# A fused attention and MLP kernel: token mixing of the first batch by head pair instead of by token tile, with the token weights transposed ahead of the first PV

## The chip, the cores and the metric

The kernel runs on one core of one Trainium2 chip. Its time is the device time of one execution in microseconds; for a kernel it is the median of several executions. The engines are called as in the profile: PE is TensorE (matmuls; PEld its weight loads), DVE is VectorE, ACT is ScalarE, POOL is GpSimd, SP is SyncE, which here only issues DMAs. POOL issues DMAs too.

## The reference

For each of 8 batches and 8 heads (576 tokens, head dimension 64) attention with a window of 32 to both sides and 8 global tokens; the result, with the heads side by side, is x (8, 576, 512). Then a residual MLP block with affine layers:

```python
scores = scale * q @ k.T ;  scores = where(mask, scores, -1e9)
mask = (abs(pos_i - pos_j) <= 32) | is_global_i | is_global_j
x  = softmax(scores) @ v                       # (8, 576, 512)
a1 = alpha1 * x + beta1
u  = x + lam * einsum('ts,bsd->btd', w_tok, a1)  # token mixing, w_tok (576, 576)
a2 = alpha2 * u + beta2
out = u + lam * (relu(a2 @ w_ch1) @ w_ch2)     # w_ch1 (512, 2048), w_ch2 (2048, 512)
```

Inputs and output are float32; the kernel multiplies in bf16 and fp16 and sums in float32.

## The kernel before

The program is one stream of instructions per engine, in the order in which the Python code issues them; waits between engines come from the tiles that they share. The order of the work is written out by hand. PSUM has eight banks of 128 x 512 float32, handed out in rings: `mlp_ps` banks 0 to 2, `sc_ps` banks 3 and 4, `pv_ps` banks 5 to 7. A ring hands a bank out again only when what was read from it before has been read, so PE waits where a copy out of a bank is late.

**Units of attention.** Heads go in four pairs (hp 0 to 3), each of 128 columns. `tr_pair` turns Q and K of a pair by PE transposes (L556) and copies them to `QP` and `KT`; `glob` picks the global columns. `sc_unit(b, hp, u)` makes a third of a pair's scores, their exp on ACT (L294, tile E), and in its last third the masked copies on DVE (PGQ, L301; PT, L306). `gk_all` and `g_rows` make the rows of the global keys (G, L249). `gq_pv` multiplies the global queries' part (RG: ACT L321, then DVE L322). `pv_x` and `pv_y` are the PV product of a pair for token tiles 0 to 2 and for tile 3 with the 64 last tokens; DVE takes the reciprocal (L347) and normalises (L354) into `XR` (tiles 0 to 3) and `SR` (the last 64 tokens). `xl_eng(b)`, which is POOL, then multiplies x by `LA1` (alpha1 times lam) into the bf16 tiles `XL` and `XL4` (L372, L398, L402), the input of token mixing.

**Token mixing.** w_tok is loaded to `WTB` and transposed to `wtT` by six `wtok_tr(k)`: five PE transposes into a bank of `mlp_ps` and one ACT copy each (L727, L729). The term of beta1 is carried by one more row: `b0_beta` writes lam times beta1 into a row of XL4 (L717, POOL), and matmuls with `ones` sum the columns of wtT into a bank (`psr`, `psr2`), from which ACT copies the sums into row 64 of chunk 4 of `wtT` and row 0 of `wt4o`. `tok_tile(b, i)` then makes one tile of 128 tokens and all 512 columns by five matmuls of 512 columns, `finish_u` adds x on DVE (L411). For batch 0 the result is transposed on PE by four float32 transposes (L418), and DVE multiplies by alpha2 (`a2c`, L420) into `UT[0]`, the input of the MLP; for the other batches POOL multiplies (L426) and a DMA transposes.

**MLP.** The 36 tiles of 128 tokens go in nine groups of four. `mlp(g)` lists 128 items: items 0 to 63 are the W1 matmuls (16 column blocks ec, four chunks cc; a chunk cc of UT is the 128 columns of a head pair), with one ReLU on ACT after each fourth (L484, with the tile `bias1`); items 64 to 127 are W2, and DVE multiplies by lam and adds u (L499, L500). `bias1` is beta2 times W1, made by 64 one-column matmuls. `weave` lays the attention of the next batch and its token mixing between the items of a group: parts are given as (units, first item, last item). For group 0 this is `first_attention(1)`, whose Q and K are cast by `cast_k` (POOL) and `cast_q` (DVE) and transposed on PE.

**The part before group 0** is a list of `run(...)` calls (L753 to L769) for batch 0, followed by the sums, the bias, the casts and token mixing (L771 to L795). POOL's queue in this part, in order: V loads of batch 1 (`load_v`, L199), the first `b0_beta`, pair 2's XL, both loads of W2 (`ld_w2`, L631), pair 3's XL, the second `b0_beta`, `cast_k`.

Of the kernel before, what the change touches and what calls it, by code (L numbers as in the profile page):

```python
# [9 lines left out]
FP32 = mybir.dt.float32  # L10
# [6 lines left out]
P = 128  # L17
# [72 lines left out]
def kernel(ctx, tc, q, k, v, global_idx, alpha1, beta1, w_tok, alpha2, beta2, w_ch1, w_ch2, lam, out):  # L90
# [78 lines left out]
    abr = T("abr", [8, P], FP32)  # L169
    a2c = T("a2c", [P, 4], FP32)  # L170
    b2c = T("b2c", [P, 4], BF16)
    ones = T("ones", [P, P], BF16)
    gbc = T("gbc", [P, 8], FP32)
    gsel = T("gsel", [P, 8], FP32)
# [178 lines left out]
        rb = bass.AP(rr.tensor, rr.offset, [rr.ap[0], [2, n], [1, 2], [0, 64]])  # L353
        nc.vector.tensor_tensor(out=xo, in0=pv[:, :, :, 0:64], in1=rb, op=ALU.mult)  # L354

    def xl_eng(b):
        return nc.gpsimd

    def pv_x(b, hp):
        st = {}  # L360

        def tile_i(i):
            def f():
                if i == 0:
                    st["ps"] = pv_ps()
                pv_mms(b, hp, i, st["ps"][:, 130 * i : 130 * i + 130])
                if i == 2:
                    base = 4 * (b % 3)
                    xo = XR[:, base : base + 3, 128 * hp : 128 * hp + 128]
                    norm(st["ps"], recip(st["ps"], 3), 0, 3, 0, P, xo.rearrange("p i (a d) -> p i a d", a=2))  # L370
                    l = LA1[:, 128 * hp : 128 * hp + 128]
                    xl_eng(b).tensor_tensor(  # L372
                        out=XL[b % 2][:, 0:3, 128 * hp : 128 * hp + 128],
                        in0=xo,
                        in1=bass.AP(l.tensor, l.offset, [l.ap[0], [0, 3], [1, 128]]),
                        op=ALU.mult,
                    )

            return (0.75, f)

        return [tile_i(i) for i in range(3)]

    def pv_y(b, hp):
        st = {}
        par = b % 2
        cs = slice(128 * hp, 128 * hp + 128)

        def f3():
            st["ps"] = pv_ps()
            pv_mms(b, hp, 3, st["ps"][:, 0:130])  # L390

        def f4():
            ps = st["ps"]
            pv_mms(b, hp, 4, ps[:, 130:260])
            xo = XR[:, 4 * (b % 3) + 3, cs]
            rt = recip(ps, 2)
            norm(ps, rt, 0, 1, 0, P, xo.rearrange("p (i a d) -> p i a d", i=1, a=2))
            xl_eng(b).tensor_tensor(out=XL[par][:, 3, cs], in0=xo, in1=LA1[:, cs], op=ALU.mult)  # L398
# [3 lines left out]
            xl_eng(b).tensor_tensor(out=XL4[par][r0 : r0 + 64, cs], in0=xo, in1=LA1[r0 : r0 + 64, cs], op=ALU.mult)  # L402

        return [(0.75, f3), (0.4, f4)]

    nub = [0]
    late = []

    def finish_u(t, ps):
        x = xs(t)  # L410
        nc.vector.tensor_tensor(out=x, in0=ps, in1=x, op=ALU.add)  # L411
        g, j = PLACE[t]
        js = slice(128 * j, 128 * j + 128)
        if t[0] == 0:

            def tail():
                for cc in range(4):
                    nc.tensor.transpose(out=ps[:, 128 * cc : 128 * cc + 128], in_=x[:, 128 * cc : 128 * cc + 128], identity=ident)  # L418
                ab = bass.AP(a2c.tensor, a2c.offset, [a2c.ap[0], [1, 4], [0, 128]])
                nc.vector.tensor_tensor(out=UT[g % 2][:, :, js], in0=ps.rearrange("p (c t) -> p c t", c=4), in1=ab, op=ALU.mult)  # L420

            late.append(tail)
            return
        ub = UB[nub[0] % 4]
        nub[0] += 1
        nc.gpsimd.tensor_tensor(out=ub, in0=x, in1=A2, op=ALU.mult)  # L426
        nc.sync.dma_start_transpose(out=UT[g % 2][:, :, js], in_=ub)

    def tok_tile(b, i):
        par = b % 2  # L430

        def f():
# [40 lines left out]
    def mlp(g):  # L473
        ut = UT[g % 2]
        a = []
        st = {}

        def w1(ec, cc):
            def f():
                if cc == 0:  # L480
                    st["ps"] = mlp_ps()
                mm(st["ps"], W1[:, cc, ec * P : (ec + 1) * P], ut[:, cc, :], cc == 0, cc == 3)
                if cc == 3:
                    nc.scalar.activation(out=HT[:, ec, :], in_=st["ps"], func=AF.Relu, bias=bias1[:, ec : ec + 1], scale=1.0)  # L484
# [24 lines left out]
        for ec in range(16):  # L509
            for cc in range(4):  # L510
                a.append(w1(ec, cc))
# [252 lines left out]
    nc.tensor.transpose(out=psb[:, 0:8], in_=abr, identity=ident[0:8, 0:8])  # L764
    nc.vector.tensor_copy(out=b2c, in_=psb[:, 0:4])
    nc.vector.tensor_copy(out=a2c, in_=psb[:, 4:8])
# [9 lines left out]
    nc.scalar.copy(out=wtT[64:65, 4, 64:576], in_=psr[64:65, :])  # L776
    nc.scalar.copy(out=wtT[64:65, 4, 0:64], in_=psr2[64:65, 0:64])
    nc.scalar.copy(out=wt4o[0:1, 64:576], in_=psr[0:1, :])
    nc.scalar.copy(out=wt4o[0:1, 0:64], in_=psr2[0:1, 0:64])
    psb = mlp_ps()  # L780
    for ec in range(16):
        for cc in range(4):
            mm(psb[:, ec : ec + 1], W1[:, cc, ec * P : (ec + 1) * P], b2c[:, cc : cc + 1], cc == 0, cc == 3)
    nc.vector.tensor_copy(out=bias1, in_=psb[:, 0:16])
# [12 lines left out]
    def first_attention(b):  # L797
# [106 lines left out]
```

The softmax here doesn't subtract the row's maximum and nothing guards it: scores larger than these inputs give would overflow.

## Time and profile before

| | us |
|---|---|
| median of 7 runs | 407.79 (406.36 to 408.64) |
| profiled execution, its own time | 407.58 |
| its span, first to last instruction | 405.7 |
| PE busy | 374.1 (92%) |
| DVE, POOL, ACT busy | 229.9, 210.8, 167.5 |
| first PV matmul starts | 31.91 |
| first token mixing matmul starts | 47.57 |
| first MLP matmul starts | 56.90 |
| first matmul of group 1 starts | 104.55 |

The span is that of the profiled execution. A row of the timeline or of the chain gives the start in microseconds from the span's beginning, the length, the engine, the line of the code (L117 is the helper `mm`, so all its matmuls have that line and are told apart by their tiles), and in brackets how long the engine stood before and who ended that. A matmul's length includes the time that its result needs to leave the array, so in a row of equal matmuls it is the distance of the starts that counts.

### The profile page before, as it was taken

How to read it: one execution, taken by the hardware profiler on the slowest of the kernel's cores; microseconds unless marked ns; L12 is line 12 of the kernel's file. 1: busy time of each engine (PE TensorE's matmuls, PEld its weight loads, DVE VectorE, ACT ScalarE, POOL GpSimd, SP SyncE). 2: the span in 40 equal slices, each digit the busy share in tenths (PEclk: the TensorE clock that was granted, in tenths of full speed). 3: DMA queues.
4: the chain of work that ended last, by engine and by line, in shares of the span. 5: the costliest groups of instructions: out<-in, count | busy, mean ns of one | idle time of the engine just before them, and what ended most of it. 6: DMA issues, size and time to landing. Idle time of an engine off the chain costs nothing.

```text
span 405.7 us, 8036 instructions
## 1 busy us (share of the span) xinstructions
PE 374.1 (92%) x3017; PEld 211.2 (52%) x3071; DVE 229.9 (57%) x621; ACT 167.5 (41%) x318; POOL 210.8 (52%) x282
## 2 busy tenths in 40 slices
PE   0658889999899999999999999999999999999996
PEld 0547556654465456545654565456545654444443
DVE  3775487579455846694569456845694565113013
ACT  2644317710573067206730772067207810540720
POOL 9534929554973994489438863894331334100000
PEclk9996899999999999999999999999999999999999
DMA  9999999992999999799949999999522003201002
GB/s 151 249 235 241 133 204 104 144 145 65 144 148 146 138 143 130 119 131 144 143 108 134 131 134 148 111 150 134 123 63 79 2 26 76 68 2 78 27 27 78
DMA packets 161690, 48.25 MB, mean 119 GB/s; under 512 B 147530, under 2 KB 154770, under 8 KB 161652
## 3 DMA queue, kind: packets, MB, share of 16 engines
q0 software_dynamic: 98752, 16.99, 60.7%
q1 hardware_dynamic: 62100, 30.36, 39.1%
q8 instruction: 24, 0.39, 0.4%
q10 hardware_dynamic: 800, 0.39, 0.4%
q14 instruction: 14, 0.11, 0.1%
HBM read 39.28 MB, written 9.44 MB: 120 GB/s over the span
## 4 chain that ended last, share of the span: by engine, by line
PE 85%; DMA 8%; DVE 3%; POOL 2%; issue 1%; ACT 1%; DVEq 0%; POOLq 0%; ACTq 0%
PE bank L117 84%; DMA XR<-in_k_dram 5%; DMA XR<-in_q_dram 3%; DVE QP L560 1%; PE bank L556 1%; POOL XL L372 0%; POOL Ve L199 0%; PE bank L418 0%; DVE OT L539 0%; POOL XL L717 0%; ACT QP L560 0%; POOL XL L402 0%; DVE XR L500 0%; POOL W L631 0%; PE bank L241 0%
## 5 line engine op out<-in xcount | busy, mean ns | idle before, releaser
L117 PE MATMUL bank<-UT,W 128*128 128x512 bf16 x545 | 153.5, 379 | 3.1 <-issue 1.1
L117 PE MATMUL bank<-W,HT 128*128 128x512 bf16 (+2 forms) x574 | 137.6, 373 | 0.8 <-issue 0.2
L484 ACT ACTIVATE HT<-bank,bias 128x512 bf16<-128x512 f32 x144 | 98.8, 687 | 66.3 <-PE bank L117 65.6
L294 ACT ACTIVATE E<-bank 128x416 f16<-128x416 f32 (+1 forms) x96 | 47.5, 514 | 122.8 <-PE bank L117 121.9
L117 PEld LDWEIGHTS <-HT 128*128 128x128 bf16 x592 | 53.4, 98 | 53.3 <-issue 1.6
L372 POOL TENSOR_TENSOR XL<-XR,LA 128x384 bf16<-128x384 f32 x32 | 32.2, 1005 | 85.5 <-DVE XR L354 55.8
L117 PEld LDWEIGHTS <-W 128*128 128x128 bf16 x640 | 50.3, 98 | 27.4 <-issue 1.8
L499 DVE TENSOR_TENSOR OT<-bank,LAM 128x512 f32<-128x512 f32 (+2 forms) x37 | 24.9, 674 | 54.8 <-PE bank L117 51.7
L117 PE MATMUL bank<-RG,G 128*128 128x65 f16 x320 | 44.4, 196 | 3.7 <-DVE RG L322 3.4
L426 POOL TENSOR_TENSOR UB<-XR,A 128x512 bf16<-128x512 f32 x28 | 35.9, 1291 | 22.2 <-DVE XR L411 15.4
L117 PE MATMUL bank<-Ve,PT 128*128 128x65 f16 x320 | 44.5, 197 | 0.0
L117 PEld LDWEIGHTS <-PT 128*128 128x128 f16 x576 | 34.0, 100 | 19.8 <-issue 3.2
L117 PE MATMUL bank<-XL,wtT 128*128 128x512 bf16 (+1 forms) x177 | 42.6, 390 | 0.6 <-POOL XL L372 0.3
L117 PEld LDWEIGHTS <-G 128*128 128x128 f16 x320 | 31.6, 99 | 15.1 <-DVE G L249 0.2
L117 PE MATMUL bank<-QP,KT 128*128 128x144 bf16 (+1 forms) x288 | 33.7, 231 | 4.5 <-ACT E L294 4.2
L117 PEld LDWEIGHTS <-KT 128*128 128x128 bf16 x288 | 25.0, 101 | 21.3 <-issue 4.8
L117 PE MATMUL bank<-Vo,PT 128*128 128x65 f16 x256 | 36.1, 195 | 0.0
L199 POOL DMA_DIRECT2D Ve<-in_v_dram x40 | 34.2, 873 | 1.8 <-DMA HT<-in_moe_w_tok_dram 1.5
L301 DVE TENSOR_TENSOR PGQ<-E,gqm 128x80 f16<-128x80 f16 x64 | 10.1, 199 | 35.4 <-ACT E L294 34.2
L354 DVE TENSOR_TENSOR XR<-bank,rd 128x384 f32<-128x384 f32 x64 | 27.2, 425 | 2.3
L500 DVE TENSOR_TENSOR XR<-OT,XR 128x512 f32<-128x512 f32 (+2 forms) x33 | 26.9, 815 | 1.6
L117 PEld LDWEIGHTS <-wtT 128*128 128x128 bf16 (+1 forms) x180 | 16.4, 102 | 20.9 <-issue 4.2
(131 smaller groups left out, 405.1 us busy)
## 6 DMA issues: line engine op xcount, KB each, us to landing
out_dram<-XR SPq DMA_DIRECT2D x31, 256.0 KB, 2.2
W<-in_moe_w_ch_dram POOLq DMA_DIRECT2D x4, 1024.0 KB, 21.1
Vo<-Ve SPq DMA_DIRECT2D x14, 260.0 KB, 3.8
Ve<-in_v_dram POOLq DMA_DIRECT2D x24, 128.0 KB, 5.4
Kb<-in_k_dram POOLq DMA_DIRECT2D x24, 128.0 KB, 5.8
Qb<-in_q_dram POOLq DMA_DIRECT2D x24, 128.0 KB, 6.9
Ve<-in_v_dram POOLq DMA_DIRECT2D x16, 96.0 KB, 5.4
XR<-in_k_dram SPq DMA_DIRECT2D x3, 512.0 KB, 16.8
```

The source lines that it names most:

```text
L117: nc.tensor.matmul(out=o, lhsT=l, rhs=r, start=st, stop=sp, skip_group_check=True)
L199: nc.gpsimd.dma_start(out=Ve[b % 2][r0 : r0 + hi - lo, c, :, 0:D], in_=v[b, :, lo:hi, :].rearrange("h p d -> p h d"))
L294: nc.scalar.activation(out=e[:, UOFF[u] : UOFF[u + 1]], in_=ps[:, 0:off], func=AF.Exp, bias=0.0, scale=0.125)
L301: nc.vector.tensor_tensor(out=pg[:, :, c0 : c0 + 16].rearrange("p c (a g) -> p c a g", a=2), in0=gq_in, in1=gq_m, op=ALU.mult)
L354: nc.vector.tensor_tensor(out=xo, in0=pv[:, :, :, 0:64], in1=rb, op=ALU.mult)
L372: xl_eng(b).tensor_tensor(out=XL[b % 2][:, 0:3, 128 * hp : 128 * hp + 128], in0=xo, in1=bass.AP(l.tensor, l.offset, [l.ap[0], [0, 3], [1, ...
L426: nc.gpsimd.tensor_tensor(out=ub, in0=x, in1=A2, op=ALU.mult)
L484: nc.scalar.activation(out=HT[:, ec, :], in_=st["ps"], func=AF.Relu, bias=bias1[:, ec : ec + 1], scale=1.0)
L499: nc.vector.tensor_tensor(out=ot, in0=ps, in1=LAM[:, lo:hi], op=ALU.mult)
L500: nc.vector.tensor_tensor(out=x, in0=ot, in1=x, op=ALU.add)
L556: nc.tensor.transpose(out=ps[:, 128 * j : 128 * j + 128], in_=quad(st_, hp, j), identity=identb)
L560: eng(out=QP[r, hp, a, 0:8, 0:64].rearrange("p t (u j) -> p t u j", j=4), in_=psq[r, 0:512].rearrange("p (j t u) -> p t u j", j=4, t=8),)
```

## The change

Batch 0's token mixing, up to the transposed MLP input, is done per head pair. `tok_first(hp)` gives two steps. `mix` makes the 128 columns of a pair for four token tiles (64 to 575) by 20 matmuls of 128 columns into one bank of `sc_ps`, and one DVE instruction adds x. `tr` transposes the four tiles on PE, and one ACT instruction scales by alpha2, adds beta2 (`b2f`) and writes chunk hp of `UT[0]`. With beta2 inside UT, group 0's ReLU takes no bias. The 64 one-column matmuls for `bias1` are moved into group 0 (`bias_mm`, at item 96). The weights are transposed earlier (groups 0 and 1 ahead of the first PV, 5 after the mixing of pair 2), the column sums before pair 2's PV. Pair 3's products with LA1 go from POOL to DVE; LA1 itself and both beta rows are made on POOL before batch 1's first loads; the Vo copies are issued ahead of G. The first nine W1 items (three column blocks, chunks 0 to 2) are issued ahead of the last pair's mixing, and in group 0 batch 1's attention is laid from item 12 instead of 4. W2 is loaded, and K is cast, after the last pair in the program's order.

```diff
-    def xl_eng(b):
-        return nc.gpsimd
+    def xl_eng(b, hp):
+        return nc.vector if (b, hp) == (0, 3) else nc.gpsimd
...
-        if t[0] == 0:
-
-            def tail():
-                for cc in range(4):
-                    nc.tensor.transpose(out=ps[:, 128 * cc : 128 * cc + 128], in_=x[:, 128 * cc : 128 * cc + 128], identity=ident)
-                ab = bass.AP(a2c.tensor, a2c.offset, [a2c.ap[0], [1, 4], [0, 128]])
-                nc.vector.tensor_tensor(out=UT[g % 2][:, :, js], in0=ps.rearrange("p (c t) -> p c t", c=4), in1=ab, op=ALU.mult)
-
-            late.append(tail)
-            return
...
+    def tok_first(hp):
+        st = {}
+        cs = slice(128 * hp, 128 * hp + 128)
+
+        def mix():
+            ps = sc_ps()
+            for i in range(4):
+                o = ps[:, 128 * i : 128 * i + 128]
+                ts = slice(64 + 128 * i, 192 + 128 * i)
+                for s in range(4):
+                    mm(o, wtT[:, s, ts], XL[0][:, s, cs], s == 0, False)
+                mm(o, wtT[:, 4, ts], XL4[0][:, cs], False, True)
+            x = XR[:, 0:4, cs]
+            nc.vector.tensor_tensor(out=x, in0=ps.rearrange("p (i c) -> p i c", i=4), in1=x, op=ALU.add)
+
+        def tr():
+            ps = sc_ps()
+            for i in range(4):
+                nc.tensor.transpose(out=ps[:, 128 * i : 128 * i + 128], in_=XR[:, i, cs], identity=ident)
+            nc.scalar.activation(out=UT[0][:, hp, :], in_=ps, func=AF.Identity, bias=b2f[:, hp : hp + 1], scale=a2c[:, hp : hp + 1])
+
+        return [(1.1, mix), (0.6, tr)]
...
-                    st["ps"] = mlp_ps()
-                mm(st["ps"], W1[:, cc, ec * P : (ec + 1) * P], ut[:, cc, :], cc == 0, cc == 3)
+                    st[ec] = mlp_ps()
+                mm(st[ec], W1[:, cc, ec * P : (ec + 1) * P], ut[:, cc, :], cc == 0, cc == 3)
                 if cc == 3:
-                    nc.scalar.activation(out=HT[:, ec, :], in_=st["ps"], func=AF.Relu, bias=bias1[:, ec : ec + 1], scale=1.0)
+                    b_ = bias1[:, ec : ec + 1] if g else 0.0
+                    nc.scalar.activation(out=HT[:, ec, :], in_=st[ec], func=AF.Relu, bias=b_, scale=1.0)
...
+        o = [(ec, cc) for ec in range(16) for cc in range(4)]
+        if g == 0:
+            o = [(ec, cc) for ec in range(3) for cc in range(3)] + [(ec, 3) for ec in range(3)] + o[12:]
...
-    run(gk_all(0, gl0_ps), act(b1_begin), act(vo0))
-    nc.vector.tensor_tensor(out=LA1, in0=LA1, in1=LAM, op=ALU.mult)
-    run(gq[0], gq[1], pv[0], sc[2][0:2], act(wtok_tr, 0), sc[2][2], pv[1], act(wtok_tr, 1), gq[2], sc[3][0:2], act(wtok_tr, 2), sc[3][2])
+    g_.tensor_tensor(out=LA1, in0=LA1, in1=LAM, op=ALU.mult)
+    b0_beta(0)
+    b0_beta(1)
+    run(act(vo0), gk_all(0, gl0_ps), act(b1_begin))
+    run(gq[0], gq[1], act(wtok_tr, 0), act(wtok_tr, 1), pv[0], sc[2][0:2], act(wtok_tr, 2), sc[2][2], act(wtok_tr, 3), pv[1], gq[2], act(wtok_tr, 4), sc[3][0:2], sc[3][2])
     for c in range(3, 5):
         load_v(1, c)
-    b0_beta(0)
-    run(pv[2], act(wtok_tr, 3), gq[3], act(wtok_tr, 4), act(wtok_tr, 5))
-    psb = pv_ps()
...
-    ld_w2(0)
-    ld_w2(1)
-    run(pv[3])
-
     psr, psr2 = mlp_ps(), mlp_ps()
     for sc_ in range(5):
         mm(psr, ones, wtT[:, sc_, 64:576], sc_ == 0, sc_ == 4)
+    nc.scalar.copy(out=wtT[64:65, 4, 64:576], in_=psr[64:65, :])
     for sc_ in range(5):
         mm(psr2[:, 0:64], ones, wtT[:, sc_, 0:64], sc_ == 0, sc_ == 4)
...
+    tk = [tok_first(hp) for hp in range(HP)]
+    run(pv[2], gq[3])
+    psb = pv_ps()
+    nc.tensor.transpose(out=psb[:, 0:8], in_=abr, identity=ident[0:8, 0:8])
+    nc.vector.tensor_copy(out=b2f, in_=psb[:, 0:4])
+    nc.vector.tensor_copy(out=a2c, in_=psb[:, 4:8])
+    run(tk[0][0], pv[3], tk[0][1], tk[1][0])
     nc.scalar.copy(out=wt4o[0:1, 64:576], in_=psr[0:1, :])
     nc.scalar.copy(out=wt4o[0:1, 0:64], in_=psr2[0:1, 0:64])
...
-    b0_beta(1)
+    nc.scalar.copy(out=wtT[64:65, 4, 0:64], in_=psr2[64:65, 0:64])
+    run(tk[1][1], tk[2][0], act(wtok_tr, 5), tk[2][1])
+    mlp0 = mlp(0)
+    for f in mlp0[0:9]:
+        f()
+    run(tk[3])
+    ld_w2(0)
+    ld_w2(1)
     for hp in range(HP):
         cast_k(hp, g_.tensor_copy)
-    for i, (w, f) in enumerate(token_mix(0)):
-        f()
-        if i > 0:
-            late[i - 1]()
-    late[3]()
     for hp in range(HP):
         cast_q(1, hp, nc.vector.tensor_copy)
+    nc.vector.tensor_copy(out=b2c, in_=b2f)
+
+    def bias_mm():
+        ps = pv_ps()
+        for ec in range(16):
+            for cc in range(4):
+                mm(ps[:, ec : ec + 1], W1[:, cc, ec * P : (ec + 1) * P], b2c[:, cc : cc + 1], cc == 0, cc == 3)
+        nc.vector.tensor_copy(out=bias1, in_=ps[:, 0:16])
...
-            parts = [(first_attention(1), 4, 94), (token_mix(1), 106, 119)]
+            for i in range(9):
+                items[i] = lambda i=i: [s() for s in slots[i]]
+        if g == 0:
+            parts = [(first_attention(1), 12, 94), ([(1.0, bias_mm)], 96, 97), (token_mix(1), 106, 119)]
```

More of the change, by code (lines that the diff above doesn't have):

```diff
@@ L171 @@
     b2c = T("b2c", [P, 4], BF16)
+    b2f = T("b2f", [P, 4], FP32)
     ones = T("ones", [P, P], BF16)
@@ L371, in f @@
                     l = LA1[:, 128 * hp : 128 * hp + 128]
-                    xl_eng(b).tensor_tensor(
+                    xl_eng(b, hp).tensor_tensor(
                         out=XL[b % 2][:, 0:3, 128 * hp : 128 * hp + 128],
@@ L397, in f4 @@
             norm(ps, rt, 0, 1, 0, P, xo.rearrange("p (i a d) -> p i a d", i=1, a=2))
-            xl_eng(b).tensor_tensor(out=XL[par][:, 3, cs], in0=xo, in1=LA1[:, cs], op=ALU.mult)
+            xl_eng(b, hp).tensor_tensor(out=XL[par][:, 3, cs], in0=xo, in1=LA1[:, cs], op=ALU.mult)
             r0 = 64 * par
@@ L401, in f4 @@
             norm(ps, rt, 1, 1, r0, r0 + 64, xo.rearrange("p (i a d) -> p i a d", i=1, a=2))
-            xl_eng(b).tensor_tensor(out=XL4[par][r0 : r0 + 64, cs], in0=xo, in1=LA1[r0 : r0 + 64, cs], op=ALU.mult)
+            xl_eng(b, hp).tensor_tensor(out=XL4[par][r0 : r0 + 64, cs], in0=xo, in1=LA1[r0 : r0 + 64, cs], op=ALU.mult)
         return [(0.75, f3), (0.4, f4)]
     nub = [0]
-    late = []
     def finish_u(t, ps):
@@ L507, in w2 @@
             return f
-        for ec in range(16):
-            for cc in range(4):
-                a.append(w1(ec, cc))
+        o = [(ec, cc) for ec in range(16) for cc in range(4)]
+        if g == 0:
+            o = [(ec, cc) for ec in range(3) for cc in range(3)] + [(ec, 3) for ec in range(3)] + o[12:]
+        for ec, cc in o:
+            a.append(w1(ec, cc))
         for j in range(4):
@@ L755 @@
     run(act(fill_pt, 1), tr[2], gl[2], sc[1][0:2], tr[3], gl[3], sc[1][2])
-    run(gk_all(0, gl0_ps), act(b1_begin), act(vo0))
-    nc.vector.tensor_tensor(out=LA1, in0=LA1, in1=LAM, op=ALU.mult)
-    run(gq[0], gq[1], pv[0], sc[2][0:2], act(wtok_tr, 0), sc[2][2], pv[1], act(wtok_tr, 1), gq[2], sc[3][0:2], act(wtok_tr, 2), sc[3][2])
+    g_.tensor_tensor(out=LA1, in0=LA1, in1=LAM, op=ALU.mult)
[3 more added lines that the diff above has]
+    run(gq[0], gq[1], act(wtok_tr, 0), act(wtok_tr, 1), pv[0], sc[2][0:2], act(wtok_tr, 2), sc[2][2], act(wtok_tr, 3), pv[1], gq[2], act(wtok_tr, 4), sc[3][0:2], sc[3][2])
     for c in range(3, 5):
         load_v(1, c)
-    b0_beta(0)
-    run(pv[2], act(wtok_tr, 3), gq[3], act(wtok_tr, 4), act(wtok_tr, 5))
-    psb = pv_ps()
-    nc.tensor.transpose(out=psb[:, 0:8], in_=abr, identity=ident[0:8, 0:8])
-    nc.vector.tensor_copy(out=b2c, in_=psb[:, 0:4])
-    nc.vector.tensor_copy(out=a2c, in_=psb[:, 4:8])
-    ld_w2(0)
-    ld_w2(1)
-    run(pv[3])
     psr, psr2 = mlp_ps(), mlp_ps()
@@ L773 @@
         mm(psr, ones, wtT[:, sc_, 64:576], sc_ == 0, sc_ == 4)
+    nc.scalar.copy(out=wtT[64:65, 4, 64:576], in_=psr[64:65, :])
     for sc_ in range(5):
         mm(psr2[:, 0:64], ones, wtT[:, sc_, 0:64], sc_ == 0, sc_ == 4)
-    nc.scalar.copy(out=wtT[64:65, 4, 64:576], in_=psr[64:65, :])
-    nc.scalar.copy(out=wtT[64:65, 4, 0:64], in_=psr2[64:65, 0:64])
+    tk = [tok_first(hp) for hp in range(HP)]
[5 more added lines that the diff above has]
+    run(tk[0][0], pv[3], tk[0][1], tk[1][0])
     nc.scalar.copy(out=wt4o[0:1, 64:576], in_=psr[0:1, :])
     nc.scalar.copy(out=wt4o[0:1, 0:64], in_=psr2[0:1, 0:64])
[L780 to L784, printed above, removed]
-    b0_beta(1)
+    nc.scalar.copy(out=wtT[64:65, 4, 0:64], in_=psr2[64:65, 0:64])
[6 more added lines that the diff above has]
+    ld_w2(1)
     for hp in range(HP):
         cast_k(hp, g_.tensor_copy)
-    for i, (w, f) in enumerate(token_mix(0)):
-        f()
-        if i > 0:
-            late[i - 1]()
-    late[3]()
     for hp in range(HP):
         cast_q(1, hp, nc.vector.tensor_copy)
+    nc.vector.tensor_copy(out=b2c, in_=b2f)
[5 more added lines that the diff above has]
+        nc.vector.tensor_copy(out=bias1, in_=ps[:, 0:16])
     nc.vector.tensor_scalar(out=hidx, in0=C32[:, 26:30], scalar1=gval[:, 0:1], scalar2=None, op0=ALU.add)
@@ L837 @@
     for g in range(9):
-        base = mlp(g)
+        base = mlp(g) if g else mlp0
         slots = [[] for _ in range(129)]
```

## The prediction

> **What bounds the kernel now.** First I read the head of the page. TensorE (PE) is busy 92% of the span, so a gain has to come from stretches in which PE waits or runs slowly.
>
> ```profile
> span 405.7 us, 8036 instructions
> PE 374.1 (92%) x3017; PEld 211.2 (52%) x3071; DVE 229.9 (57%) x621; ACT 167.5 (41%) x318; POOL 210.8 (52%) x282
> ```
>
> Second, the windows view, cut where the granted PE clock changes. Columns: stretch, length, busy us (instructions) of PE, PEld, DVE, ACT, POOL, granted clock, DMA share, GB/s.
>
> ```profile
> 27.10:30.50 3.40, 1.64 (x17) 1.13 (x15) 2.31 (x6) 1.09 (x3) 0.82 (x1) 1.00 1.11 237
> 31.90:37.40 5.50, 5.49 (x76) 5.06 (x76) 2.67 (x12) 1.97 (x4) 1.82 (x3) 0.50 1.12 237
> 37.40:40.80 3.40, 2.97 (x56) 2.44 (x55) 1.85 (x8) 2.82 (x7) 2.79 (x5) 1.00 1.42 250
> 40.80:44.20 3.40, 2.54 (x44) 2.05 (x46) 2.66 (x12) 2.06 (x4) 3.26 (x4) 1.00 2.96 156
> 44.20:47.60 3.40, 2.96 (x75) 2.30 (x74) 1.30 (x5) 1.37 (x4) 3.38 (x6) 1.00 1.69 74
> 47.60:51.00 3.40, 3.18 (x8) 1.21 (x9) 0.69 (x1) 0.00 (x0) 3.40 (x6) 0.50 1.15 162
> 56.90:62.00 5.10, 4.31 (x51) 2.71 (x53) 4.95 (x14) 2.62 (x5) 3.05 (x5) 1.00 0.95 161
> 62.00:103.40 41.40, 41.03 (x367) 23.58 (x370) 30.01 (x88) 17.32 (x34) 25.92 (x32) 1.00 1.19 118
> ```
>
> From 62 us on PE is full: work put there costs its whole time, and what starts it earlier is won for good. The place to win is 28.5 to 56.9, where the clock is halved twice (31.9 to 37.4 and 47.6 to 51.0). Each comes after a 3.4 us stretch with little array work: 1.64 us, and one in which 2.0 us of the 2.96 are the one-column bias matmuls. Stretches with 2.54 and 2.97 kept full clock.
>
> Third, the chain of waits from 39 to 58 us (start, length, what):
>
> ```profile
> 39.83 1.67 POOL Ve L199 x2
> 41.57 1.27 POOL XL L717
> 42.91 1.00 POOL XL L372
> 44.73 0.71 POOL W L631
> 46.51 1.02 POOL XL L372
> 48.35 3.22 PE bank L117 x8
> 54.72 0.70 DVE XR L411
> 55.46 0.67 PE bank L418 x4
> 56.16 0.69 DVE UT L420
> ```
>
> GpSimd (POOL) carries it: V loads, a beta row, pair 2's XL, the issue of both W2 loads, pair 3's XL; only then does token mixing start (47.57), at half clock, and the last tile still runs add, transposes, copy before the first MLP matmul at 56.90. The normalised pair 3 was ready for POOL at 44.76; its XL began 1.75 us later, behind the W2 issues.
>
> Fourth, the timeline at the first PV and at the batch 1 transposes:
>
> ```profile
> 28.52 0.83 DVE L249 TENSOR_TENSOR G<-EG,GM 128x1024 f16<-128x1024 f16 x2 [1.03 <-ACT EG L274]
> 31.91 0.21 PE L117 MATMUL bank<-RG,G 128*128 128x65 f16 x1 [2.64 <-DVE RG L322]
> 58.00 0.39 PE L556 MATMUL bank<-identb,UT 128*128 128x128 bf16 x4
> 58.22 0.38 PE L117 MATMUL bank<-UT,W 128*128 128x512 bf16 x1
> ```
>
> PE stands 2.64 us because DVE does G, both Vo copies (1.40) and LA1 (0.69) before RG.
>
> **The change, part by part.** *First PV.* LA1 goes to POOL (about 1.3, as L426 of the same size), which idles before 22.46 until PE releases TSB; both inputs have landed by 19.4 (LAM: issued 8.37, 11.0 to land). Both beta rows (2 x 1.26, L717) follow, once their 2 KB loads behind A2 (9.19 + 12.3) are in, 21.5 to 24. Queued behind them on POOL are batch 1's tail and V loads: about 1.5 us later, and who waits for them, SP's Vo copies, ran only at 48. Vo on DVE moves into the 1.03 us gap before G (27.49 to 28.9), so G ends 29.74 and RG 29.99. PE fills with two token-weight transpose groups (0.36 each from the row's 0.40 with its tail); w_tok had landed at 27.4 (issued 9.98, 17.4 to land). PV 0 starts at 30.0 instead of 31.91. The G product is 0.4 later than before and the RG 1.6 earlier: the three DVE steps behind G are gone.
>
> *Pairs 1 to 3.* ScalarE (ACT) now orders it: copies of weight groups 0 and 1 (0.62 each), exps 0.46 and 0.45, copy 0.62, exp 0.50: pair 2's exps end 33.3 (before 36.08). DVE: masks 1.13 (L301 0.31, L306 0.82), norms of pair 1 1.53 (0.20, 0.57, 0.18, 0.30, 0.28), RG 0.29, to 36.3. ACT: copy, RG, copy, three exps, to 36.6. The five column-sum matmuls (5 x 0.216) run at 35.9, their row copy ends 37.8. PV 2 37.1 to 38.0; norms and RG 3 to 39.7, b2f and a2c to 40.0.
>
> *Mixing by pair.* Per pair 20 matmuls of 128 columns instead of 5 of 512 per tile: same columns, 80 weight loads instead of 20. The row nearest is the transposes at 58.00: four of 128 columns, each with its own load, and PE's next matmul starts at 58.22, so 55 ns each and 20 x 56 = 1.13 us; 5 x 0.216 = 1.08 before. The Trainium skill ("TensorE: Matmul & The Clock Gate", Back-to-back issue gap) speaks against it: about 81 ns for each of a stream of load and 128-column matmul pairs. By that, 80 x 25 ns would be 2.0 us more and the end 407.7; this trace's row says otherwise and I go by it.
>
> Then: mix 0 38.8 to 39.9 (it waits for the small transpose, that for a bank of pair 2's norm at 38.7); add 0.69 to 40.8; PV 3 39.9 to 40.8; DVE on pair 3: norms 1.53 and the three XL products, not shown on DVE before. L500, two SBUF inputs of 128x512, takes 0.69 at best, so 0.52 + 2 x 0.2 = 0.92 (bounds 0.5, and POOL's 1.9), to 43.3; add 1 to 44.0. PE stands 1.5 us from 42.5, since the transposes of pair 1 are next in its queue and mix 2 waits behind them. Transposes 0.44 (four float32 ones, 51.41 to the next matmul at 51.85), mix 2 1.13, end latency 0.17, add 0.69: 46.5. Transposes, UT copy on ACT (0.69, row of L484; L420 on DVE cost 0.68) to 47.9. Nine W1 matmuls, the third waiting for that copy, to 49.4. Mix 3 1.13, add, transposes, copy with latencies 2.2: item 9 starts at 52.9, all at full clock.
>
> *Clock.* Between 40.8 and 44.2 PE has some 1.9 us of work, nearer to the 1.64 that turned cold than to 2.54. One half-clock stretch over transposes and mix 2 costs 1.4: 54.3. Bounds: 52.9 (none) and 55.8 (two, badly placed). The skill (same page, What's actually happening) gives a free-running window of 3413 ns, at half rate after an idle one; trace stretches of 5.5 and 3.4 us agree, and by it the place differs from run to run.
>
> *Gain at the start of the MLP:* item 0 began at 56.90; now item 9 at 54.3, nine matmuls (1.94) done: 56.90 - 54.3 + 1.94 = 4.5.
>
> *Bias.* The 64 one-column matmuls ran 45.29 to 47.28 under POOL's wait, hence free. In the loop at slot 96 nothing covers them: 2.0 lost. If they fall into one 3.4 us stretch a half-clock one follows: 1.7 more; chance (3.4 - 2.0)/3.4 = 0.42, so I take 0 and keep 1.7 for the range.
>
> *Start of the loop.* Three ReLUs follow each other (2.07), so batch 1's first K copy waits about 1 us for ACT and bank release for the second transpose pair with it; DVE in turn is ahead. Before, PE lost 0.8 there; I add 0.5 (0 to 1.5). POOL: load_v(1,4) still waits until 40.6 for the first W1 load, then pair 2's XL to 43.3 (needed 44.7), W2 issued at 43.3 instead of 44.68, K casts after it. W2 needs 12.7 to 16 us and is first used near 77: covered. Attention in 82 slots instead of 90 and ReLU without its bias tile I cost at 0: PE is full there and ACT busy 42%; uncovered, the denser slots would add to the 0.5, inside its 1.5. SP's queue is not moved past. The wt4o and wtT row copies (0.57, 0.2, 0.2) lie on ACT at 42.2 to 43.2 while it waits for PE.
>
> *Sum:* 4.5 - 2.0 - 0.5 = 2.0 (rounded) off the profiled run's own 407.58 (span 405.7 and 1.9 around it): 405.5. The median is 0.2 above that run: 405.7.
>
> **The rivals.** *More:* no half-clock stretch in the new prologue, cheap XL: 4.0 + 1.94 - 2.0 - 0.5 = 3.4, and up to 1 more from the 1.12 us wait at 103.42 for group 1's input: 402.5 to 404. For: PE gets work in each gap. Against: 1.5 us standing at 42.5. *No change:* the bias matmuls drop the clock in the full loop as they did at 47.6: 2.0 - 1.7 = 0.3, 407.4. For: that very row. Against: the 0.42 above. *Slower:* the clock again, everywhere. Prologue work is cut into pieces between ACT and DVE steps, and each 3.4 us stretch with under about 1.7 us of array work costs 1.4 to 1.7. Without any the gain is 3.4; from three stretches (prologue and bias together) it is lost, and with four at 1.6 it is -3.0: 410.8. For: half of the stretches before were so. Against: the array has 17 us of work in 24, where 2.54 of 3.4 sufficed.
>
> **How the numbers follow.** Forecast 0.52 (403.7 to 406.5), more 0.14, no change 0.18, slower 0.16. Changes under 0.3% (1.2 us) count as none, about what measurement can tell. So faster 0.66, same 0.18, slower 0.16. Leaving out some 0.08 below and 0.11 above, the range is 403.0 to 409.2.
>
> **What would show it.** Right: first PV near 30; XL of pair 3 on DVE near 0.5; mix near 1.1 per pair at full clock; the first relu near 55 (57.98 before); 64 one-column matmuls for 2 us near 95; end 2 us earlier. Wrong: mix at 1.6, half clock in three or more stretches, or PE idle above 1.5 us in the loop's first 5 us.

## The result, and the profile after

The changed kernel takes 410.09 us in the median (407.56 to 411.98, 15 runs), against 407.81 for the kernel before (405.83 to 408.73, 36 runs). The ratio is 1.0063, with a 95% interval of 1.0045 to 1.0082: slower by 0.6%. The prediction was 405.7, with a range of 403.0 to 409.2 and faster as the likeliest sign.

The profiled execution of the changed kernel spans 3.4 us more than that of the kernel before, with the same PE work:

```profile
span 409.1 us, 8161 instructions
PE 374.2 (91%) x3077; PEld 213.2 (52%) x3131; DVE 232.0 (57%) x620; ACT 169.1 (41%) x322; POOL 211.1 (52%) x280
```

The windows view, columns as before, shows where PE was slow or stood:

```profile
40.80:44.20 3.40, 3.10 (x60) 2.79 (x57) 2.84 (x10) 0.37 (x1) 3.25 (x6) 1.00 2.83 140
44.20:47.60 3.40, 1.30 (x22) 1.11 (x20) 3.26 (x7) 1.54 (x4) 3.40 (x5) 1.00 1.81 120
47.60:51.00 3.40, 2.39 (x19) 2.36 (x20) 0.86 (x2) 0.78 (x1) 0.12 (x1) 0.52 1.20 175
51.00:54.40 3.40, 2.94 (x18) 2.16 (x18) 0.69 (x1) 1.13 (x2) 0.00 (x0) 0.50 1.06 232
```

From 44.2 to 47.6 PE has 1.30 us of work while DVE (3.26) and POOL (3.40) are full; two half-clock stretches follow. What fills DVE there, and what already came late, is in the timeline of the same execution (start, length, engine, line, tiles):

```profile
20.00 1.71 POOL L772 TENSOR_TENSOR LA<-LA,LAM 128x512 f32<-128x512 f32 x1 [4.10 <-DMA LAM<-in_moe_lam_dram]
21.78 3.01 POOL L733 TENSOR_TENSOR XL<-UB,LAM 1x512 bf16<-1x512 f32 x2
...
20.51 1.37 DVE L302 TENSOR_TENSOR PGQ<-E,gqm 128x80 f16<-128x80 f16 x2
21.80 1.88 DVE L307 TENSOR_TENSOR PT<-E,mask 128x640 f16<-128x640 f16 x2
...
31.15 0.73 PE L117 MATMUL bank<-Ve,PGQ 128*128 128x130 f16 x10 [0.53 <-ACT EG L275]
...
44.40 1.68 DVE L373 TENSOR_TENSOR XL<-XR,LA 128x384 bf16<-128x384 f32 x1
46.53 0.72 DVE L399 TENSOR_TENSOR XL<-XR,LA 128x128 bf16<-128x128 f32 x1
47.48 0.38 DVE L403 TENSOR_TENSOR XL<-SR,LA 64x128 bf16<-64x128 f32 x1
...
45.03 2.69 POOL L552 CAST UT<-XR 128x512 bf16<-128x512 f32 x4
...
48.61 1.09 PE L450 MATMUL bank<-ident,XR 128*128 128x128 f32 x4 [3.11 <-DVE XR L445]
...
59.83 0.38 PE L117 MATMUL bank<-UT,W 128*128 128x512 bf16 x1 [0.87 <-ACT UT L451]
```

The same instructions in the kernel before:

```profile
20.74 0.30 DVE L301 TENSOR_TENSOR PGQ<-E,gqm 128x80 f16<-128x80 f16 x2
20.95 0.82 DVE L306 TENSOR_TENSOR PT<-E,mask 128x640 f16<-128x640 f16 x2
...
28.54 0.73 PE L117 MATMUL bank<-Ve,PGQ 128*128 128x130 f16 x10 [0.53 <-ACT EG L274]
```

Two places. At 20.5 the masked copies of pair 0 (1.12 us as two pairs in the kernel before, 20.74 to 21.77) take 3.2 us while POOL makes LA1 and the beta rows; the global queries' product starts at 31.15 instead of 28.54, and the first PV matmul at 32.63, where the prediction had 30.0. At 44.4 pair 3's products on DVE take 1.68 + 0.72 + 0.38 = 2.78 us; POOL's K casts run beside them from 45.03, and PE stands 3.11 us. Item 9 starts at 59.83; the prediction had 54.3.

### The profile page after: what moved, and what is told of

Same layout as the page of the kernel before. It is cut to its first block, busy times and chain, and to the rows that moved or that the text cites. A ratio compares the mean times of both kernels' runs of the same rounds, so it can differ in the third digit from the quotient of the medians.

```text
span 409.1 us, 8161 instructions
## 1 busy us (share of the span) xinstructions
PE 374.2 (91%) x3077; PEld 213.2 (52%) x3131; DVE 232.0 (57%) x620; ACT 169.1 (41%) x322; POOL 211.1 (52%) x280
## 4 chain that ended last, share of the span: by engine, by line
PE 83%; DVE 7%; DMA 4%; issue 2%; ACT 1%; POOL 1%; SPq 0%; DVEq 0%; POOLq 0%; ACTq 0%
PE bank L117 82%; DMA XR<-in_q_dram 4%; DVE QP L216 1%; DMA UT<-UB 1%; PE bank L450 1%; DVE XR L445 1%; DVE XR L355 1%; DVE PT L307 1%; DVE XR L514 1%; DVE OT L513 1%; DVE QP L576 1%; DVE XR L411 0%; ACT E L295 0%; DVE PGQ L302 0%; DVE XL L373 0%
## 5 line engine op out<-in xcount | busy, mean ns | idle before, releaser
L498 ACT ACTIVATE HT<-bank,bias 128x512 bf16<-128x512 f32 x128 | 87.7, 686 | 52.8 <-PE bank L117 52.0
L117 PEld LDWEIGHTS <-HT 128*128 128x128 bf16 x592 | 53.3, 98 | 52.9 <-issue 1.6
L373 POOL TENSOR_TENSOR XL<-XR,LA 128x384 bf16<-128x384 f32 x31 | 31.1, 1002 | 83.7 <-DVE XR L355 56.5
L117 PE MATMUL bank<-RG,G 128*128 128x65 f16 x320 | 43.0, 193 | 0.4
L117 PE MATMUL bank<-Ve,PT 128*128 128x65 f16 x320 | 43.2, 194 | 0.0
L117 PE MATMUL bank<-XL,wtT 128*128 128x512 bf16 (+2 forms) x238 | 42.5, 334 | 0.1
L117 PEld LDWEIGHTS <-PT 128*128 128x128 f16 x576 | 32.6, 98 | 16.5
L117 PEld LDWEIGHTS <-G 128*128 128x128 f16 x320 | 30.7, 97 | 14.5
L117 PE MATMUL bank<-Vo,PT 128*128 128x65 f16 x256 | 34.9, 192 | 0.0
L302 DVE TENSOR_TENSOR PGQ<-E,gqm 128x80 f16<-128x80 f16 x64 | 11.2, 216 | 33.9 <-ACT E L295 33.9
L117 PEld LDWEIGHTS <-wtT 128*128 128x128 bf16 (+1 forms) x240 | 19.8, 104 | 17.9 <-issue 1.7
```

Of the source, the lines that this page charges most:

```text
L117: nc.tensor.matmul(out=o, lhsT=l, rhs=r, start=st, stop=sp, skip_group_check=True)
L302: nc.vector.tensor_tensor(out=pg[:, :, c0 : c0 + 16].rearrange("p c (a g) -> p c a g", a=2), in0=gq_in, in1=gq_m, op=ALU.mult)
L373: xl_eng(b, hp).tensor_tensor(out=XL[b % 2][:, 0:3, 128 * hp : 128 * hp + 128], in0=xo, in1=bass.AP(l.tensor, l.offset, [l.ap[0], [0, 3], ...
L498: nc.scalar.activation(out=HT[:, ec, :], in_=st[ec], func=AF.Relu, bias=b_, scale=1.0)
```

## The experiments

Theory A: a DVE instruction with both inputs in SBUF is held while POOL runs an elementwise instruction, and POOL by DVE; the change moves POOL work beside such DVE work twice. Theory B: the loss lies in the new structure (mixing by pair, bias matmuls in the full loop), or in the clock alone. Each ratio below is to the kernel before on the same chip. The experiments ran on three chips (the first four on one, the next four on another, the last two on a third), so across them ratios are compared rather than medians.

**LA1 and the beta rows later.**

```diff
-    g_.tensor_tensor(out=LA1, in0=LA1, in1=LAM, op=ALU.mult)
-    b0_beta(0)
-    b0_beta(1)
...
         ld_tail(q, TSB, g_, 1, 64)
+        g_.tensor_tensor(out=LA1, in0=LA1, in1=LAM, op=ALU.mult)
+        b0_beta(0)
...
         cast_k(hp, g_.tensor_copy)
+    b0_beta(1)
```

> Edit: POOL makes LA1 and the first beta row after batch 1's two tail loads (about 23.9 to 26.5 us) instead of ahead of them (20.0 to 24.8), the second beta row after the K casts. Theory A: a DVE instruction with two inputs in SBUF waits for the POOL instruction that runs, so the masks at 20.5 to 23.7 (L302 pair 1.37, L307 pair 1.88) lost 2.1 us to LA1 and the betas. A expects them back at 0.31 and 0.82, the first global-query matmul at 28.5 instead of 31.15 and 2.0 to 3.5 us less than the changed kernel: 406.6 to 408.1. Theory B: the loss is in mixing by pair and the bias matmuls in the full loop, and the late start is a load's or PE's clock's: masks stay slow or the start stays near 31, time within 0.8 of 410.1.

Measured: 405.78 us (405.36 to 406.39), ratio 0.9951 (0.9936 to 0.9967). The tile view of the masks gives minimum, median and maximum of one instruction in ns; first the changed kernel, then this one:

```profile
L302 DVE TENSOR_TENSOR PGQ<-E,gqm x2: 186/720/1255, 20.5 to 21.7; 128x80 f16<-128x80 f16 x2
...
L307 DVE TENSOR_TENSOR PT<-E,mask x2: 478/978/1479, 21.8 to 22.2; 128x640 f16<-128x640 f16 x1, 128x512 f16<-128x512 f16 x1
```

```profile
L302 DVE TENSOR_TENSOR PGQ<-E,gqm x2: 183/188/193, 21.1 to 21.2; 128x80 f16<-128x80 f16 x2
...
L307 DVE TENSOR_TENSOR PT<-E,mask x2: 417/450/482, 21.3 to 21.7; 128x640 f16<-128x640 f16 x1, 128x512 f16<-128x512 f16 x1
...
L373 DVE TENSOR_TENSOR XL<-XR,LA x1: 559/559/559, 42.5 to 42.5; 128x384 bf16<-128x384 f32 x1
```

In the changed kernel one of each pair was held for about 1 us and the other ran at its usual length: a wait, not a slower rate. The first PGQ product, from 20.51, ended at 21.76, just behind LA1 (21.71), and the second took 0.19. The edit won more than A expected (4.3 us between the medians, 2.0 to 3.5 expected), and the last line says why: with the start 2.3 us earlier, pair 3's products ran from 42.5 to 44.3, ahead of the K casts at 45.01, and escaped the second collision as well. That POOL's own loads were late is not the reason: batch 1's V loads are issued later here (26.84) than in the changed kernel (26.16). This profile by itself does not show what the edit is worth, since in it LAM landed only at 21.2; its twelve times do, and the reverse test in the kernel before, further down.

**Pair 3's products on POOL.**

```diff
-        return nc.vector if (b, hp) == (0, 3) else nc.gpsimd
+        return nc.gpsimd
```

> Edit: pair 3's three products with LA1 on POOL again, all else as changed. Theory A: on DVE they took 1.68 + 0.72 + 0.38 = 2.78 beside POOL's W2 issues and K casts (0.92 estimated) and held the add of pair 1 until 47.79. A expects the add near 45.2, the products about 1.9 on POOL in the open, W2 issued 1.9 later and not missed, 2 to 3.5 us less: 406.6 to 408.1, with fewer half-clock stretches between 44 and 55. Theory B: no change beyond 0.8 of 410.1, since PE's standing comes from the order of the pairs.

Measured: 406.40 (404.63 to 407.74), ratio 0.9975 (0.9957 to 0.9994). That is 0.0088 or 3.6 us less than the changed kernel, just above A's 2 to 3.5, and B's "no change" does not hold. POOL makes the three products from 42.30 to 44.12, the add of pair 1 starts at 43.46, and no stretch from 30 to 62 us has half clock. The profiled execution, with 404.63 the fastest of the twelve, shows the other thing that decides, the landing of LAM:

```profile
21.48 1.42 POOL L772 TENSOR_TENSOR LA<-LA,LAM 128x512 f32<-128x512 f32 x1 [5.58 <-DMA LAM<-in_moe_lam_dram]
```

Here LAM landed 13.0 us after its issue (11.6 in the changed kernel's profile), POOL started when the masks (20.7 to 21.8) were all but done, and the first global-query product came at 28.88. Whether the first collision happens is thus a matter of one DMA's landing. This edit does nothing about it, so the profile shows a kernel without either collision, and how many of the twelve executions had the first is not known.

**Both edits.** The diffs are those above.

> Edit: both edits together (LA1 and first beta row after the tail loads, pair 3's products on POOL). Theory A: the two losses lie one behind the other on the path, so they add: 4 to 6.5 us less than the changed kernel, 403.6 to 406.1, faster than the kernel before (407.8). Theory B: 409 to 410. If only the clock counted, one of the two edits would already give all of it and the sum would be that of one: 407.

Measured: 405.40 (404.69 to 405.87), ratio 0.9942 (0.9920 to 0.9964). Faster than the kernel before, as A said; but not the sum of the two, and not to be told from the first edit alone (0.9951). That edit removes the second collision too, as its last line shows; the second edit's profile escaped the first collision by LAM's landing. These three runs alone do not rule out that only the clock counts, which expected as much: in all three profiles the granted clock is 1.00 from 30 to 62 us, so each edit brought the clock back as well. The runs with the K casts on ACT and with PE kept warm, below, separate the two. Part of the gain over the kernel before is the clock's too: of that kernel's 32 times on this chip, the nine with a mean granted clock of 0.996 have a median of 406.4 us and the seventeen with 0.987 one of 408.1.

**K casts on ACT.**

```diff
-    for hp in range(HP):
-        cast_k(hp, g_.tensor_copy)
...
+    for hp in range(HP):
+        cast_k(hp, nc.scalar.copy)
     run(tk[1][1], tk[2][0], act(wtok_tr, 5), tk[2][1])
```

> Edit: the four K casts of batch 1 on ACT, behind the wt4o copies where it stands idle, instead of on POOL; pair 3's products stay on DVE and POOL still issues both W2 loads at 43.2 to 45.0. Theory A, casts hold DVE: L373 falls from 1.68 to 0.5 to 0.6, the three products from 2.78 to 0.9 to 1.1, the add of pair 1 to about 46.0, 1.5 to 2.5 us less: 407.6 to 408.6. Theory A', the issue of the loads holds DVE as well: L373 stays at 1.0 to 1.2 (held until 45.0), products at 1.5, 1 us less. Theory B: the products are slow on DVE by themselves, 2.78 stays and 410.1.

Measured: 407.08 (405.28 to 407.66), ratio 0.9981 (0.9963 to 0.9998). Pair 3's products and POOL beside them, from the timeline:

```profile
45.06 0.56 DVE L373 TENSOR_TENSOR XL<-XR,LA 128x384 bf16<-128x384 f32 x1
...
46.07 0.29 DVE L399 TENSOR_TENSOR XL<-XR,LA 128x128 bf16<-128x128 f32 x1
...
45.30 0.89 POOL L647 DMA_DIRECT2D W<-in_moe_w_ch_dram  x1 [0.47 <-DMA TSB<-in_k_dram]
```

The products fall to 0.56 + 0.29 + 0.28 = 1.13, although POOL issues a W2 load in the middle of them. So the casts held DVE, and issuing a DMA did not. The many mask products that run beside POOL's load issues say the same: in the profile of the kernel before, 12 of the 128x512 ones took 417 to 420 ns there and 20 with POOL idle 412 to 420. The products are not slow on DVE by themselves. The gain, 3.0 us between the medians, is more than the 1.5 to 2.5 expected: the first collision is still there (global queries' product at 31.81), but PE's wait is shorter and the clock stays at 1.00.

**The same POOL work in the kernel before.**

```diff
+    g_.tensor_tensor(out=OT[0], in0=LA1, in1=LAM, op=ALU.mult)
+    b0_beta(0)
+    b0_beta(1)
     run(gk_all(0, gl0_ps), act(b1_begin), act(vo0))
```

> Edit of the kernel before: three POOL instructions are added at the place where the change put them, ahead of batch 1's tail loads: a product of LA1 and LAM into a tile that nobody reads then, and both beta rows a first time (they are made again later). Nothing else moves. Theory A (DVE waits for the running POOL instruction): masks of pair 0 (L301, L306) lose 1.5 to 2 us whenever LAM has landed before 21, the first PV matmul goes from 31.9 to about 34, and the time rises by 1 to 2.5 us over the kernel before: 408.8 to 410.3. Theory B: the idle POOL has room for them, no change: 407.0 to 408.5.

Measured: 409.74 (408.32 to 410.80), ratio 1.0060 (1.0039 to 1.0082). Three instructions on an idle engine, whose results change nothing, cost what the whole change costs. The first PV matmul starts at 35.03 instead of 31.91 (about 34 expected). The masks in the tile view:

```profile
L301 DVE TENSOR_TENSOR PGQ<-E,gqm x2: 187/722/1257, 21.0 to 22.2; 128x80 f16<-128x80 f16 x2
...
L306 DVE TENSOR_TENSOR PT<-E,mask x2: 478/977/1476, 22.3 to 22.7; 128x640 f16<-128x640 f16 x1, 128x512 f16<-128x512 f16 x1
```

**PE kept warm.** The changed kernel with idle work for PE in the gap of 3.11 us.

```diff
     run(tk[0][0], pv[3], tk[0][1], tk[1][0])
+    for i in range(12):
+        mm(psb, ones, wtT[:, 0, 64:576], True, True)
```

> Edit of the changed kernel: 12 matmuls of 512 columns whose result nobody reads go to PE behind the mixing of pair 1, where PE stood 3.1 us for DVE. Both waits on DVE stay. If the clock is a cost of its own, the stretches of 47.6 to 54.4 stay at full clock and the second mix falls from 2.34 to 1.3, transposes from 1.09 to 0.66: 2 to 3.5 us less than the changed kernel in executions with the late start, 406.6 to 408.3. If only DVE's waits count, PE does useless work and the time stays within 0.8 of 410.1.

Measured: 408.75 (407.75 to 409.97), ratio 1.0042 (1.0024 to 1.0059). Both collisions are still there (products 0.75 + 0.75 + 0.38, the global queries' product at 31.39), and the clock stays up:

```profile
47.60:51.00 3.40, 2.92 (x35) 2.30 (x34) 0.90 (x2) 1.40 (x2) 0.08 (x1) 1.00 1.29 201
51.00:54.40 3.40, 2.96 (x24) 1.72 (x23) 0.00 (x0) 0.79 (x2) 0.00 (x0) 1.00 1.12 156
```

Its profiled span is 406.7 against 409.1. Of these 2.4 us some 0.7 came ahead of the clock, since pair 3's products were held for less here (1.88 us instead of 2.78, the add of pair 1 at 47.13 instead of 47.79); from that add to the end of the span it is 1.7 us, which is what the two half-clock stretches cost in that execution. In the medians the gain is smaller, 1.0063 to 1.0042 or 0.9 us, with intervals that overlap; not every execution has these stretches. Of the changed kernel's 15 times, the six with a mean granted clock of 0.998 or more are 407.56 to 409.08 us, the nine with less 409.84 to 411.98. The expected 2 to 3.5 us was too much. A part of the loss is the clock's, as a consequence of DVE's delay, and without it the kernel is still slower than before.

**Without the bias matmuls**, from the kernel with both edits.

```diff
-        ps = pv_ps()
-        for ec in range(16):
-            for cc in range(4):
-                mm(ps[:, ec : ec + 1], W1[:, cc, ec * P : (ec + 1) * P], b2c[:, cc : cc + 1], cc == 0, cc == 3)
-        nc.vector.tensor_copy(out=bias1, in_=ps[:, 0:16])
+        nc.vector.memset(bias1, 0.0)
```

> Edit of the kernel with both edits (405.4): the 64 one-column matmuls in group 0 are left out and the bias of groups 1 to 8 is zero, so beta2 is missing there. As the prediction has it, their 2.0 us lie on the full path and nothing follows from them for the clock: 403.0 to 403.8. If they also drop the clock in part of the executions: up to 1.7 more, 401.7 to 403. If the loop hides them, 405 to 405.6.

Measured: 403.30 (403.13 to 404.22), ratio 0.9910 (0.9890 to 0.9931): 0.9942 less 0.9910 is 0.32%, 1.3 us, with overlapping intervals, and the medians differ by 2.1. That fits 2.0 on the full path and no further clock cost, but does not fix it to better than about 1 us. The two profiles put it at 1.6: from item 9 to the first matmul of group 1 they take 47.79 and 46.19 us.

**Pair 3 mixed ahead of the nine W1 matmuls**, from the kernel with both edits.

```diff
-    for f in mlp0[0:9]:
-        f()
-    run(tk[3])
+    tk[3][0][1]()
+    for f in mlp0[0:4]:
+        f()
+    tk[3][1][1]()
+    for f in mlp0[4:9]:
+        f()
```

> Edit of the kernel with both edits (405.4): pair 3's mixing goes ahead of the nine W1 matmuls, and its transposes behind the fourth of them, so that its add, transposes and copy run beside the matmuls. There PE stands from about 47.9 to 48.4 and from 51.9 to 54.4 but for the transposes. Expected: first ReLU at 52 to 52.5 instead of 54.8 and 2 to 2.8 us less, 402.6 to 403.4. If the loop's start is bound by DVE's casts and Q copies, which then start earlier too, 1 us less at least; if the wait moves to UT's bank or W1, nothing.

Measured: 402.99 (402.12 to 403.22), ratio 0.9891 (0.9870 to 0.9912). PE now goes without a stop from pair 3's mixing to the MLP:

```profile
48.49 1.28 PE L117 MATMUL bank<-XL,wtT 128*128 128x128 bf16 x20
49.61 1.03 PE L117 MATMUL bank<-UT,W 128*128 128x512 bf16 x4
50.63 0.66 PE L450 MATMUL bank<-ident,XR 128*128 128x128 f32 x4
51.12 1.89 PE L117 MATMUL bank<-UT,W 128*128 128x512 bf16 x8
```

The first ReLU starts at 52.62 instead of 54.78.

**Only the start of the change**, in the kernel before.

```diff
         ld_tail(q, TSB, g_, 1, 64)
+        g_.tensor_tensor(out=LA1, in0=LA1, in1=LAM, op=ALU.mult)
+        b0_beta(0)
...
-    run(gk_all(0, gl0_ps), act(b1_begin), act(vo0))
-    nc.vector.tensor_tensor(out=LA1, in0=LA1, in1=LAM, op=ALU.mult)
+    run(act(vo0), gk_all(0, gl0_ps), act(b1_begin))
...
-    b0_beta(0)
```

> Edit of the kernel before: only the start of the change, in the form without contention. Both Vo copies go ahead of G on DVE, LA1 and the first beta row go to POOL behind batch 1's tail loads; mixing by tile, the bias matmuls and the order of the transposes stay. If the gap of 2.64 us ahead of the first PV is the gain of the whole change, it keeps most of what the kernel with both edits won (405.4): the first PV at 30 instead of 31.9, 1.5 to 2.5 us less than before, 405.3 to 406.3. If POOL's chain behind it (V loads, XL, W2) decides, the earlier PV is lost again there, but the beta row leaves that chain: 0.5 to 1.3 us less, 406.5 to 407.3. Then mixing by pair brings the rest.

Measured: 407.26 (404.56 to 408.69), ratio 0.9986 (0.9965 to 1.0007): no difference that can be told. The first PV matmul starts at 30.64 instead of 31.91, and POOL gives a part of that back:

```profile
42.37 0.93 POOL L631 DMA_DIRECT2D W<-in_moe_w_ch_dram  x1 [1.20 <-DMA W<-in_moe_w_ch_dram]
44.77 0.89 POOL L631 DMA_DIRECT2D W<-in_moe_w_ch_dram  x1 [1.47 <-DMA TSB<-in_k_dram]
45.67 1.01 POOL L372 TENSOR_TENSOR XL<-XR,LA 128x384 bf16<-128x384 f32 x1
```

The issues of W2 now wait for earlier loads to land, and pair 3's XL waits behind them: it starts at 45.67 instead of 46.51, and the first MLP matmul at 56.06 instead of 56.90. So of 1.27 us at the first PV 0.84 are left at the MLP in this profile, and in the times nothing that can be told. The gain comes with the rest of the change. That holds mixing by pair, and also W2 issued behind pair 3 in the program's order; no run separates these two.

**Bias matmuls in a gap of the mixing**, from the version with pair 3 ahead.

```diff
     run(tk[0][0], pv[3], tk[0][1], tk[1][0])
+    psw = pv_ps()
+    for ec in range(16):
+        for cc in range(4):
+            mm(psw[:, ec : ec + 1], W1[:, cc, ec * P : (ec + 1) * P], b2c[:, cc : cc + 1], cc == 0, cc == 3)
+    run(tk[1][1])
+    nc.vector.tensor_copy(out=bias1, in_=psw[:, 0:16])
```

> Edit of the kernel that mixes pair 3 ahead of the nine W1 matmuls (403.0): the 64 one-column bias matmuls go from group 0's loop to the place between the mixing and the transposes of pair 1, where PE stands 0.94 us for DVE's add. Of their 2.0 us about 0.9 would lie in the gap and 1.1 ahead of the transposes: 0.5 to 0.9 us less, 402.1 to 402.5. If they make that stretch poor in array work and the clock halves behind it: 1.0 to 1.7 more than that, 403.1 to 404.2.

Measured: 401.27 (400.74 to 401.77), ratio 0.9843 (0.9814 to 0.9872), the fastest version: 1.6% faster than the kernel before. The gain over the version with pair 3 ahead, 0.48% or 2.0 us by the ratios (with intervals that just overlap, on two chips), is more than the 0.5 to 0.9 expected. The matmuls took 1.6 us:

```profile
43.40 1.74 PE L117 MATMUL bank<-b2c,W 128*128 128x1 bf16 x64
45.01 0.64 PE L450 MATMUL bank<-ident,XR 128*128 128x128 f32 x4
```

About 1.1 us of that was idle time of PE: the transposes of pair 1 start 1.34 us after the start of that pair's add (43.67), where it was 0.84 in the version with pair 3 ahead (44.50 to 45.34). The clock stays at 1.00 there: 3.02 us of PE work lie in the stretch of 44.2 to 47.6.

## Why the prediction was wrong

The sum leaves out that DVE and POOL can hold each other, and the changed kernel makes them meet twice. Item 9 came 5.5 us later than predicted (59.83, not 54.3). It also came 5.5 later than in the profile with LA1 later (54.37), and there the parts can be read off: 1.87 at pair 0's add (42.98 and 41.11), from the late start; 1.65 more at pair 1's transposes (48.61 and 45.09), from pair 3's products (2.78 and 1.13); 1.94 more after that, with PE at half clock. Step by step:

- *First PV, the step that failed first.* The prediction put LA1 and the beta rows on an idle POOL and asked only who was queued behind them on POOL. Who works beside them was not asked: the masks of pair 0 on DVE lost 2.1 us, and the global queries' product came 2.6 later (28.54 to 31.15). Some 0.7 of that is PE at its slow rate for longer: the 320-column matmuls ahead of it start 0.267 us apart to their end (30.15), in the kernel before only until 27.17 and then 0.136 apart. The kernel with these instructions later (405.78) and the kernel before with them added (409.74) show it from both sides.
- *Pair 3's XL on DVE, mis-sized.* 0.92 was taken from the shortest length of a DVE row (L500), with bounds 0.5 and 1.9. It took 2.78 beside the K casts and 1.13 beside DMA issues only. The upper bound came from POOL's speed and had no room for a wait. The warning stood in the kernel before: L500 takes 0.69 us there with POOL idle and up to 1.71 beside POOL's products of the same size.

```profile
98.18 1.26 POOL L426 TENSOR_TENSOR UB<-XR,A 128x512 bf16<-128x512 f32 x1 [0.33 <-DVE XR L411]
98.73 1.26 DVE L500 TENSOR_TENSOR XR<-OT,XR 128x512 f32<-128x512 f32 x1
```

- *Clock.* One half-clock stretch was taken, at some 1.9 us of PE work in 3.4; there were two (47.6 to 54.4), since DVE's delay left PE with 1.30 us of work in 3.4. Without that delay 1.9 would not have been too little: 1.76 us of work in a stretch (51.27 to 54.68 with LA1 later) kept full clock. The bound for two, 55.8, held only with the two other steps right: it was 59.83. The first half-clock stretch of the kernel before is 6.9 us long (twice 3.4), from 30.5 to 37.4, not 5.5: PE stood through its first 1.4.
- *Mixing by pair: right.* In the changed kernel's profile pair 0's 20 matmuls start at 41.58 and PE's next one at 42.71, 1.13 us as predicted. The 81 ns that the Trainium skill ("TensorE: Matmul & The Clock Gate", Back-to-back issue gap) gives for a matmul of 128 columns in such a stream would make it 1.6, an estimate that this row does not bear out.
- *Bias: right in kind,* 1.6 in the profiles where 2.0 was taken. *Start of the loop:* item 9 to group 1 took 59.83 to 107.59, 47.8 us; the prediction's terms make 47.65 - 1.94 + 2.0 + 0.5 = 48.2.

With the two collisions away the times are 405.78 and 405.40, close to the forecast of 405.7, and the profile with LA1 later has item 9 at 54.37 (54.3 predicted). That is in part luck: the forecast holds 1.4 us for a half-clock stretch that this profile does not have, and the rest of its prologue took 1.5 us longer than the 52.9 that the prediction gives at full clock. None of the three signs of being wrong that the prediction named appeared: the mix took 1.13, two stretches had half clock, and PE stood 1.3 us in the loop's first 5. They looked where the sum had terms. Of the rivals, *more* adds up to 403.4 to 404.4 by its own terms (407.8 less 3.4, and up to 1 more), not 402.5 to 404, and did not happen; *slower* had the right sign and almost the right end (410.8), but through the clock alone, in three to four stretches; there were two, and the run with the clock kept up is still slower than before. *No change* through the bias matmuls did not happen: the clock stayed at 1.00 behind them in the changed kernel's profile.

The Trainium skill has a rule that the prediction should have weighed: "SBUF — State Buffer", Who interferes with whom, says that a DVE instruction with two inputs in SBUF contends with a GpSimd instruction that reads SBUF, by an exclusive lock on a shared pair of ports. The runs agree that the two hold each other: of two equal mask products one took 186 ns and the other 1255. The same section reports that `tensor_tensor`, unlike `tensor_copy`, did not stall DMAs that GpSimd issues, and infers that issuing needs the write interface, which `tensor_tensor` does not take. The run with the casts on ACT fits that, seen from the other side: L373 took 0.56 us beside a W2 issue. The ports themselves no run here shows.

What stays open: in which order the two engines take turns, and how often the collisions occur over many executions, since only profiled ones show them. On the order: the first PGQ product was held until LA1 ended, but the first PT product, issued 0.02 us after a beta row, took its usual 0.48 while the beta row took 1.61 instead of 1.26, and the second PT product was held. And L373 of the changed kernel would by its usual length have ended at 44.96, just ahead of the recorded start of the first K cast (45.03); that the casts held it rests on the run without them. That the kernel's 407.56 to 411.98 shrinks to 405.36 to 406.39 with the later LA1 fits a collision that comes and goes with LAM's landing, but was not counted.

## What to carry to other kernels

Before work goes to an idle POOL, list the DVE instructions with two SBUF inputs that run in the same microseconds: an idle engine is not free when it shares a way to memory with a busy one. A price read from the shortest length of a row is a lower bound; look up what its longer ones ran beside, and what will run beside the new one. And when two edits each win nearly all, look whether one of them moves the other's collision out of the way before adding them up.

## What the runs showed of the hardware that was not expected

- A DVE product that takes 0.19 us alone took 1.26 beside POOL's LA1, one of 0.42 (128x512, fp16) took 1.48 beside the beta rows; POOL's LA1 went from 1.30 to 1.71 (to 2.06 in another profile) and the first beta row from 1.26 to 1.61. A one-partition row held DVE as a full tile did.
- A change of 1.4 us in the landing of one 256 KB load (LAM, 11.6 to 13.0 us) went with whether 2 us were lost: in the four profiles with LA1 or its copy ahead of the tail loads and started at 20.0 to 20.3 the masks took 3.2 us, in the one where it started at 21.48 they took 1.12.
- Of the stretches of 3.4 us at full clock, counted from the changes of the granted clock, those with 0.69, 0.73, 1.17 and 1.59 us of PE work were followed by half clock, those with 1.76 (twice) and 1.95 were not. Two with more work, 2.97 and 2.10, were followed by half clock all the same; both hold one-column bias matmuls.
- 64 one-column matmuls in the gap of the mixing left the clock at 1.00, where the same 64 in a poor stretch of the kernel before were followed by half clock.
